# Threshold attention and SwiGLU: plain weight stores moved to later slots, with new transfer times and tables for the first batches

## The chip, the cores and the metric

The kernel runs on one core of a Trainium2 chip. The core has a matrix engine (TensorE, PE in the profile; its weight loads are PEld), a vector engine (VectorE, DVE), a scalar engine (ScalarE, ACT), a general engine (GpSimd, POOL) and SyncE (SP), which here only issues DMAs. Each engine takes its instructions in the order of the program and waits for the others by semaphores. The metric is the device time of one execution in microseconds; the median of several runs counts.

## What is computed

Eight batches of eight heads, with 576 tokens of 64 values a head. The attention keeps only the scores within tau of the largest of their row; its output is the input of a SwiGLU block with 512 inputs, 1536 hidden values and 512 outputs. All in float32.

```python
scores = scale * np.matmul(q, k.transpose(0, 1, 3, 2))
thresh = np.max(scores, axis=-1, keepdims=True) - tau
scores = np.where(scores >= thresh, scores, -1000000000.0)
scores = scores - np.max(scores, axis=-1, keepdims=True)
attn = np.exp(scores)
attn = attn / (np.sum(attn, axis=-1, keepdims=True) + 1e-09)
x = np.matmul(attn, v)               # then heads side by side: 4608 x 512
g = x @ w_gate
silu = g * (1.0 / (1.0 + np.exp(-g)))
out = (silu * (x @ w_val)) @ w_out
```

## The kernel before

**Head and slots.** The first batch is worked off by an older scheme (up to about 140 us), in which the weights are also fetched and brought to float32 form. After it the program is a chain of 84 slots. Seven batches have four pairs of heads each, and a pair takes three slots. In every slot PE computes scores (L1514) for a third of the queries of two heads. DVE takes the row maxima (L1535, L1537), the halves of a row are exchanged (by ACT, L1549, or by DVE, L1543), ACT takes exponentials (L1560), and DVE masks them and sums the rows (L1562). The reciprocal of the sum (L1576) scales the tiles, on ACT (L1588) or on POOL (L1585), and DVE transposes them (L1590). The scores lie in two PSUM tiles; the next slot's scores can start when the masks have read them. In the second slot of a pair PE first works off the attention products of the pair before (L1611).

**Loads.** In the first slot of a pair the q and k of the pair after it are loaded (L336, eight DMAs of 72 KB from SP); POOL scales q (L1650), DVE transposes k (L1652) and q (L1655). In the second slot v is loaded (L380).

**Work that fills a slot.** Between a slot's scores and the next, PE is given pieces of the SwiGLU block of the batch before. Batch 0 is done by plain products (`plain_group`, L1040, one step is eight matmuls of one matrix). Batches 1 and on use a Winograd form of Strassen's product with seven products instead of eight: six groups of columns (`Group`, L940, steps p1, p5, p2, p6, p3, p7, p4; after the first group p4 follows the next group's p1). The hidden values are multiplied with w_out in seven output products a half (`Outputs`, L1106; batches 0 and 1) or by a nested form (L1308, L1320; later batches).

**Sums of weights.** For the seven products each group needs three sums of weight blocks. POOL makes them in slots 4 to 9 (`weight_sums`, L795), and SP stores them to HBM (L847, 768 KB a group). A fourth sum replaces a weight block in place (`weight_part`, slots 10 to 15). In batch 1 a group takes four plain blocks from SBUF and its three sums from a ring of two places, to which they are loaded from HBM (`load_sums`, L867; the load for group g + 2 is asked for at p4 of group g). From batch 2 on all seven blocks of a group are streamed from HBM (`load_flow`, L873). For this the four plain blocks of each group have to be stored to HBM once as well: `store_plain` (L862), four DMAs of 256 KB a group. In this kernel it is called in slot 10 + g for group g.

**What sets the order.** A planner (`Plan`) keeps modelled clocks of the engines. Each operation is a job with an engine, a modelled duration, the jobs it depends on, a rank, and for DMAs two more values: `lag`, the time from issue to landing, and `moves`, the time that its bytes occupy the DMA engines; transfers with `moves` are queued one behind the other in the account. The planner emits jobs in the order in which they could start by the account, so a modelled time changes the order of the instructions on an engine, never what they do. PE's order is written by tables: how many steps a slot gets.

- `PLAIN` (slots 0 to 7): plain product steps of batch 0.
- `CH0` (slots 8 to 12): output products of batch 0.
- `GV` (slots of a batch from its second): group steps. One table for all batches.
- `CH`, `CD`: output products; `CH` for batches 0 and 1, of which the last rows fall into the first two slots of the batch after.
- `FIRST_POOLED`, `FIRST_MAX_BY_ACT` (slots 0 to 23): how many of the three tiles of the second head POOL scales, and in which slots ACT exchanges the maxima. `POOLED` and `MAX_BY_ACT` serve the later batches.

SP's queue is shared by all of this: q, k and v loads, the stores of sums and of plain blocks, the loads of the ring, the output. A DMA that waits on SP holds up all behind it.

Of the kernel before, what the change touches and what calls it, by code (L numbers as in the profile page):

```python
# [27 lines left out]
class Plan:  # L28
# [12 lines left out]
    def job(self, eng, took, fn, *deps, rank=1, lag=0.0, moves=0.0):  # L41
        j = Job(eng, took, fn, rank, lag, moves)
        for d in deps:
            if isinstance(d, Job) and d.end is None:
                d.then.append(j)
                j.waits += 1
            elif d is not None:
                j.ready = max(j.ready, self.after(d, eng) if isinstance(d, Job) else d + self.HOP)
        if not j.waits:
            self.open[eng].append(j)  # L50
        return j
# [61 lines left out]
def kernel(  # L113
# [11 lines left out]
    nc = tc.nc  # L125
# [15 lines left out]
    NU3 = 3  # L141
# [4 lines left out]
    NF2, DM2 = NF // 2, DM // 2  # L146
# [27 lines left out]
    HW = 2 * TC  # L174
# [15 lines left out]
    ring = big[:, 2 * NCC * DFF:].rearrange("p (s n) -> p s n", s=2)  # L190
# [11 lines left out]
    sums_hbm = hbm.tile([NF2, P, GW], F32, name="sums_hbm")  # L202
# [523 lines left out]
    plan = Plan()  # L726
    job, pe = plan.job, plan.pe
# [53 lines left out]
    def pair_cols(w, kh, g):  # L781
        return w[:, 2 * kh:2 * kh + 2, g * TC:(g + 1) * TC]
# [3 lines left out]
    SUM_AT = 2  # L786
# [7 lines left out]
    def pool_tt(out, a, b, op):  # L794
        return lambda: nc.gpsimd.tensor_tensor(out=out, in0=a, in1=b, op=op)  # L795
# [43 lines left out]
    stores, summed_g, parts = {}, {}, []  # L839

    def weight_sums(g, place, *deps):
        t1, t2, t4 = (place[:, n * HW:(n + 1) * HW].rearrange("p (k f) -> p k f", k=2) for n in range(3))
        w11, w12, w21, w22 = pair_cols(wval, 0, g), pair_cols(wgat, 0, g), pair_cols(wval, 1, g), pair_cols(wgat, 1, g)
        j = job("POOL", 1.3, pool_tt(t1, w12, w11, ALU.subtract), *deps, rank=3)
        j = job("POOL", 1.3, pool_tt(t2, w22, t1, ALU.subtract), j, rank=3)
        j = job("POOL", 1.3, pool_tt(t4, w21, t2, ALU.subtract), j, rank=3)
        stores[g] = job("SP", 0.1, lambda: nc.sync.dma_start(  # L847
            out=sums_hbm[g][:, SUM_AT * HW:(SUM_AT + 3) * HW], in_=place), j, lag=4.0)
        summed_g[g] = j

    def weight_part(g, *deps):
# [6 lines left out]
    def store_plain(g, *deps):  # L858

        js = []  # L860
        for n, w in ((0, pair_cols(wval, 0, g)), (1, pair_cols(wval, 1, g)), (5, pair_cols(wgat, 1, g)), (6, pair_cols(wgat, 0, g))):
            js.append(job("SP", 0.1, lambda n=n, w=w: nc.sync.dma_start(  # L862
                out=sums_hbm[g][:, n * HW:(n + 1) * HW].rearrange("p (k f) -> p k f", k=2), in_=w), *deps, lag=4.0))
        plain_stores[g] = js

    def load_sums(c, g, *deps):
        loads[c, g] = job("SP", 0.1, lambda: nc.sync.dma_start(  # L867
            out=ring[:, g % 2], in_=sums_hbm[g][:, SUM_AT * HW:(SUM_AT + 3) * HW]), stores[g], *deps, lag=4.0)

    def load_flow(c, g, part, *deps):  # L870
        lo, to = ((0, 4), (4, NQ))[part]
# [157 lines left out]
    def plain_group(t, g, n_bufs):  # L1029

        x = xts["full", t]

        def mul(mat, name):
            hold = take(name)

            def fn():
                ps = hold.rows()
                for i in range(2):
                    for c in range(NCC):
                        nc.tensor.matmul(ps[:, i], wgv[:, mat, c, (2 * g + i) * P:(2 * g + i + 1) * P], x[:, c, :],  # L1040
                                         start=(c == 0), stop=(c == NCC - 1))

            return hold, pe(2 * NCC * MM, fn, *hold.deps)

        hold, m = mul(0, "pg")
        (u, u_old), (n, n_old) = turn_of(u_bufs), turn_of(n_bufs)
        ps = hold.rows()
        tj = job("ACT", 0.6, lambda: nc.scalar.activation(n.ap, ps, AF.Tanh, scale=0.5), m, *n_old, rank=1)
        cj = job("ACT", 0.6, lambda: nc.scalar.activation(u.ap, ps, AF.Copy, scale=0.5), m, *u_old, rank=1)
        hold.read_by(tj, cj)  # L1050
        hold.done(False)
        yield
        hold, m = mul(1, "pv")
        ht, pv = hall[:, t, g], hold.rows()
        vj = job("DVE", 0.7, lambda: nc.vector.scalar_tensor_tensor(out=ht, in0=n.ap, scalar=1.0, in1=pv, op0=ALU.add, op1=ALU.mult),
                 tj, m, rank=1)
        n.jobs = [vj]
        hold.read_by(vj)
        hold.done(False)
        gated[0, t, g] = mj = job("POOL", 1.3, pool_tt(ht, ht, u.ap, ALU.mult), vj, cj, rank=1)  # L1060
        u.jobs = [mj]
        yield
# [634 lines left out]
    def end_gates():  # L1697
        state.pop("last_product")()

    def gv_steps(n):  # L1700
        for _ in range(n):
            next(state["gv"])
# [6 lines left out]
    NS = NU3 * NP  # L1709
    LAST_GV, LAST_PLAIN = 9, 8  # L1710
    GV = {1: 2, 2: 7, 3: 4, 4: 5, 5: 6, 6: 5, 7: 6, 8: 6, 9: 0}
    CH = {0: 2, 1: 5, 9: 1, 10: 3, 11: 2}
    POOLED = {1: 3, 3: 2, 6: 3, 7: 2, 11: 1}
    MAX_BY_ACT = (0, 3, 5, 6, 8, 9, 10)
    FIRST_POOLED = {0: 2, 1: 3, 3: 2, 4: 3, 6: 1, 7: 2, 8: 1, 10: 2, 11: 1, 12: 2, 13: 2, 16: 2, 17: 1, 19: 3, 20: 1, 22: 3, 23: 2}
    FIRST_MAX_BY_ACT = (1, 3, 5, 6, 9, 12, 14, 15, 17, 18, 20, 21, 23)
    CD = {0: 1, 1: 1, 9: 2, 10: 2, 11: 2}
    PLAIN = {0: 1, 1: 3, 2: 2, 3: 2, 4: 2, 5: 3, 6: 1, 7: 2}
    CH0 = {8: 3, 9: 2, 10: 4, 11: 3, 12: 2}

    def begin_outputs(c):
# [6 lines left out]
    def block_part(b, kk):  # L1728
        s = (b - 1) * NS + kk
        if s == 0:  # L1730
            state["gv"] = chain(*(plain_group(0, g, u_bufs) for g in range(IN_HEAD, NF2)), *(plain_group(1, g, n_bufs) for g in range(NF2)))
        if s <= NS:
            gv_steps(PLAIN.get(s, 0))
            if s == 2:
                first, state["run"] = outputs(0)
                first.half_sums(plan.t)
            elif s == LAST_PLAIN:
                next(state["gv"], None)
            out_steps(CH0.get(s, 0))
            return  # L1740
        c = b - 1
        if kk < 2 and state["run"]:
            out_steps((CH if c - 1 < DEEP else CD).get(kk, 0))
        if kk in GV:
            if kk == 1:
                state["gv"] = gates_and_values(c)
            gv_steps(GV[kk])
            if c == DEEP and kk <= len(NESTED):
                deepen(NESTED[kk - 1], plan.t, *(j for js in plain_stores.values() for j in js), *summed)
            if kk == LAST_GV:  # L1750
                next(state["gv"], None)
                begin_outputs(c)
                if c < DEEP:
                    out_steps(1)
                    end_gates()
        if kk >= LAST_GV:
            out_steps((CH if c < DEEP else CD).get(kk, 0))

# [3 lines left out]
    for s, (n, x) in enumerate((n, x) for n in range(len(halved)) for x in range(NU3)):  # L1762
        seg = halved[n]
        i, t = seg["i"], seg["tiles"][x]
        b, kk = s // NS + 1, s % NS
        if x == 1 and n > 0:
            prepare_v(seg, attend(halved[n - 1]))
        pss, mark = slot_scores(seg, t)
        if s == 0:
            next(last, None)  # L1770
            attend_tile()
            next(last, None)
            flip()
            plan.t += 2.4
            plan.free.update(DVE=2.0, ACT=2.5)
        elif s == 1:
            attend_tile()
            next(last, None)
            plan.t += 1.0
            store_last(0)  # L1780
        if s == 1:
            prepare_v(seg)
        at_, pooled, max_by_act = (kk, POOLED, MAX_BY_ACT) if b > DEEP else (s, FIRST_POOLED, FIRST_MAX_BY_ACT)
        slot_rest(seg, t, pss, mark, pooled.get(at_, 0), at_ in max_by_act, 1 if x == NU3 - 1 else 2)
        if x == 0 and n + 1 < len(halved):
            prepare_next(i + 1, plan.t)
        if s == 0:
            joins = rest_of_weights()
        block_part(b, kk)
        if 2 <= s < 6:  # L1790
            output_sums(s - 2, plan.t, *joins)
        if s in WS:
            g, place = WS[s]
            weight_sums(g, place, plan.t, *joins, stores.get({2: 0, 3: 1, 4: 3, 5: 4}.get(g)))
        if 10 <= s < 10 + NF2:
            g = s - 10
            weight_part(g, summed_g[g], plan.t)
            store_plain(g, parts[g])

    tail[0] = True  # L1800
    out_steps(1)
# [13 lines left out]
    for c in (B - 1, B):  # L1815
# [4 lines left out]
        if c < B:  # L1820
            w = SM // 2
            j = []
# [40 lines left out]
```

## Time and profile before

| what | value |
|---|---|
| median of 3 runs | 1403.74 us (1401.99 to 1404.30) |
| the profiled execution: time, span | 1406.35 us, 1404.5 us |
| mean granted clock of TensorE | 0.994 |
| matmuls: scores, group steps, attention, plain and output products | L1514, L940, L1611, L1040, L1106 |
| DMAs of SP: ring and stream loads (big<-sums_hbm) | 90, of 768 or 1024 KB |
| DMAs of SP: plain stores (sums_hbm<-big, 256 KB) | 24 |
| HBM read, written | 138.28 MB, 21.50 MB |

Slots 0, 13 and 26 begin at 140.89, 285.08 and 452.14 us of the span. The times of single instructions are from one profiled execution, whose span is the time from its first to its last instruction; 1.9 us of the device time lie outside it. Where a row names a releaser in brackets, the engine was idle before the instruction for that long, and the releaser is what ended the wait.

### The profile page before, as it was taken

Reading aid. Unit: us, or ns where it says so; the run is one execution under the profiler, and the core shown is the slowest. Engines: PE = TensorE matmul, PEld = TensorE weight load, DVE = VectorE, ACT = ScalarE, POOL = GpSimd, SP = SyncE. Lnnn points to the kernel's source line nnn. Section 1 sums busy time; section 2 is a strip of 40 time slices with the busy share of each in tenths; the row PEclk is TensorE's granted clock in tenths of the full one; section 3 lists DMA queues with packets and bytes.
Section 4 is the critical chain, followed back from the end, with each engine's and each line's share of the span. In section 5 each row is a group of like instructions: output and inputs, shape, how many; then the busy total and the mean of one; then the engine's idle time right before and its main releaser. Section 6 shows DMA issues by size and latency. Waiting matters only on the chain.

```text
span 1404.5 us, 38812 instructions
## 1 busy us (share of the span) xinstructions
PE 1365.8 (97%) x15486; PEld 1118.0 (80%) x15486; DVE 1023.4 (73%) x2680; ACT 867.4 (62%) x2257; POOL 693.3 (49%) x641
## 2 busy tenths in 40 slices
PE   9998999979999999999999999999999999999997
PEld 6666777758777778877888888887887788899897
DVE  7978888867787677787778777877777764365365
ACT  6878676666665677667667766776677773221320
POOL 2456598743375659733874378436943592000000
PEclk9999999999999999999999999999999999999999
DMA  7824305545324551545146523553065404424411
GB/s 170 217 93 154 82 19 142 185 131 139 81 77 114 140 140 36 165 127 146 35 131 157 144 58 108 146 142 93 27 196 141 110 26 151 144 78 143 152 51 31
DMA packets 208388, 162.30 MB, mean 116 GB/s; under 512 B 166224, under 2 KB 180560, under 8 KB 202832
## 3 DMA queue, kind: packets, MB, share of 16 engines
q1 hardware_dynamic: 204608, 159.39, 40.2%
q8 instruction: 123, 2.02, 0.6%
q10 hardware_dynamic: 3600, 0.43, 0.2%
q14 instruction: 57, 0.47, 0.1%
HBM read 138.28 MB, written 21.50 MB: 114 GB/s over the span
## 4 chain that ended last, share of the span: by engine, by line
PE 77%; DVE 1%; SPq 1%; issue 1%; DMA 0%; POOL 0%; ACT 0%; DVEq 0%; ACTq 0%
PE pb L940 17%; PE pa L940 12%; PE pe L940 12%; PE px L1308 11%; PE sc L1514 8%; PE xa L1611 8%; PE py L1320 5%; PE po L1106 3%; PE sc L940 1%; SPq L336 1%; DVE big L798 0%; PE sc L1308 0%; SPq L1370 0%; DVE hall L993 0%; DMA sums_hbm<-big 0%
## 5 line engine op out<-in xcount | busy, mean ns | idle before, releaser
L1562 DVE SCALAR_TENSOR_TENSOR pall<-sc,th,pall 128x288 f32<-128x288 f32 x504 | 243.6, 513 | 64.5 <-ACT pall L1560 50.4
L940 PE MATMUL pb<-xall,big 128*128 128x256 f32 x1080 | 256.5, 380 | 0.0
L1560 ACT ACTIVATE pall<-sc,nm 128x288 f32<-128x288 f32 x504 | 231.7, 497 | 34.3 <-DVE pall L1562 33.9
L1590 DVE STREAM_TRANSPOSE pall<-pall 128x576 f32<-128x576 f32 x252 | 189.1, 763 | 62.6 <-ACT pall L1588 44.2
L940 PEld LDWEIGHTS pb<-xall,big 128*128 128x128 f32 x1080 | 203.7, 190 | 29.9 <-issue 2.7
L1588 ACT ACTIVATE pall<-pall,ri 128x288 f32<-128x288 f32 x416 | 189.7, 526 | 24.6 <-DVE ri L1576 24.1
L795 POOL TENSOR_TENSOR hall<-hall,tmp 128x512 f32<-128x512 f32 x80 | 102.3, 1279 | 167.0 <-DVE hall L993 157.7
L940 PE MATMUL pa<-xall,big 128*128 128x256 f32 x768 | 183.4, 382 | 0.0
L940 PE MATMUL pe<-xall,big 128*128 128x256 f32 x752 | 179.2, 381 | 0.2 <-POOL xall L795 0.2
L1514 PE MATMUL sc<-kT,qT 64*32 64x144 f32 (+1 forms) x5376 | 153.6, 350 | 15.2 <-DVE pall L1562 10.3
L940 PEld LDWEIGHTS pa<-xall,big 128*128 128x128 f32 x768 | 143.9, 190 | 22.8 <-issue 3.4
L940 PEld LDWEIGHTS pe<-xall,big 128*128 128x128 f32 x752 | 141.8, 190 | 22.1 <-issue 2.7
L1514 PEld LDWEIGHTS sc<-kT,qT 64*32 64x32 f32 x5376 | 100.9, 107 | 69.4 <-issue 31.3
L1535 DVE TENSOR_REDUCE mx<-sc 128x2 f32<-128x576 f32 x168 | 124.4, 740 | 35.4 <-PE sc L1514 35.0
L1611 PE MATMUL xa<-pall,vall 64*32 64x288 f32 x4032 | 133.7, 404 | 1.8 <-issue 1.0
L1585 POOL TENSOR_SCALAR pall<-pall,ri 128x288 f32<-128x288 f32 x88 | 88.1, 1013 | 68.7 <-DVE ri L1576 56.9
L1611 PEld LDWEIGHTS xa<-pall,vall 64*32 64x32 f32 x4032 | 76.0, 107 | 52.7 <-issue 9.2
L1570 ACT COPY sums<-sums 32x6 f32<-32x6 f32 x336 | 66.6, 198 | 45.5 <-DVE pall L1562 40.9
L992 ACT ACTIVATE vall<-tmp 128x512 f32<-128x512 f32 x96 | 60.4, 629 | 55.2 <-DVE tmp L1005 29.9
L1320 PE MATMUL py<-wo,hall 128*128 128x256 f32 x336 | 74.8, 379 | 0.0
L1549 ACT COPY mx<-mx 32x6 f32<-32x6 f32 x192 | 37.3, 194 | 60.5 <-DVE mx L1537 58.6
L1537 DVE TENSOR_REDUCE mx<-sc 128x1 f32<-128x288 f32 x168 | 74.4, 443 | 0.0
(225 smaller groups left out, 2326.9 us busy)
## 6 DMA issues: line engine op xcount, KB each, us to landing
big<-sums_hbm SPq DMA_DIRECT2D x42, 1024.0 KB, 5.3
big<-sums_hbm SPq DMA_DIRECT2D x48, 768.0 KB, 4.7
vall<-in_v_dram SPq DMA_DIRECT2D x112, 144.0 KB, 3.1
out_dram<-big SPq DMA_DIRECT2D x32, 256.0 KB, 3.5
qT<-in_q_dram SPq DMA_DIRECT2D x112, 72.0 KB, 4.8
kT<-in_k_dram SPq DMA_DIRECT2D x112, 72.0 KB, 3.0
wo<-in_moe_w_gate_dram SPq DMA_DIRECT2D x16, 384.0 KB, 3.8
wo<-in_moe_w_val_dram SPq DMA_DIRECT2D x16, 384.0 KB, 4.6
```

The source lines that it names most:

```text
L795: return lambda: nc.gpsimd.tensor_tensor(out=out, in0=a, in1=b, op=op)
L940: nc.tensor.matmul(ps[:, i], w[:, k_, i * P:(i + 1) * P], x[:, k_, :], start=first and i == k_ == 0, stop=True, skip_group_check=True)
L1308: nc.tensor.matmul(ps, a[:, f, :], ws[n][:, f, :], start=bank_ not in begun, stop=True, skip_group_check=True)
L1320: nc.tensor.matmul(ps, a[:, f, i * P:(i + 1) * P], operands[o][:, f, :], start=first and i == f == 0, stop=True, skip_group_check=True)
L1514: nc.tensor.matmul(pss[h][(slice(g * G, (g + 1) * G), *part)], qT[hs, col:col + G], kT[hs, c * SH + keys[0]:c * SH + keys[1]], start=True, ...
L1535: rs.append(job("DVE", 0.72, lambda n=n, tile_=tile_: nc.vector.tensor_reduce(out=mx[:, n:n + 2, 0], in_=tile_[:, :, 0:SH], axis=AX.X, op= ...
L1560: ej = job("ACT", 0.42, lambda x=x, n=n: nc.scalar.activation(ps[x], scs[x], AF.Exp, bias=nm[:, n:n + 1]), ej, *((masks[h, 0], masks[h, 1] ...
L1562: masks[x] = job("DVE", 0.45, lambda x=x, n=n: nc.vector.scalar_tensor_tensor(out=ps[x], in0=scs[x], scalar=th[:, n:n + 1], in1=ps[x], op0 ...
L1585: scaled.append(job("POOL", 1.02, lambda x=x, n=n: nc.gpsimd.tensor_scalar(out=x, in0=x, scalar1=ri[:, n:n + 1], scalar2=None, op0=ALU.mul ...
L1588: scaled.append(job("ACT", 0.46, lambda x=x, n=n: nc.scalar.activation(x, x, AF.Copy, scale=ri[:, n:n + 1]), rj, rank=rank))
L1590: seg["turned"].append(job("DVE", 0.72, lambda both=both: nc.vector.transpose(out=both, in_=both), *scaled, rank=rank))
L1611: nc.tensor.matmul(holds[a].ap()[x * G:(x + 1) * G, 0:SH].rearrange("d (i q) -> d i q", q=G), vr[rs, h, j, ds], p[rs, h, :, j, :], start=( ...
```

## The change

Three things are changed. Plain blocks are stored later: group g is no longer stored in slot 10 + g, but groups 0 to 5 in slots 13, 14, 16, 17, 19 and 20, which are the slots of batch 1 that load no q and k. The account of the planner gets other values for the stores and loads of sums (shorter `lag`, and `moves`, which they lacked), and 0.6 us of issue for a plain store. The tables are written anew: `GV_FIRST` serves batch 1 in place of `GV`; `CH`, `PLAIN`, `FIRST_POOLED` and `FIRST_MAX_BY_ACT` have other entries. The sums of the PE tables are the same as before: 41 group steps, 16 plain steps, 14 output products a batch.

```diff
@@ weight_sums
         stores[g] = job("SP", 0.1, lambda: nc.sync.dma_start(
-            out=sums_hbm[g][:, SUM_AT * HW:(SUM_AT + 3) * HW], in_=place), j, lag=4.0)
+            out=sums_hbm[g][:, SUM_AT * HW:(SUM_AT + 3) * HW], in_=place), j, lag=2.0, moves=3.4)
@@ store_plain
-            js.append(job("SP", 0.1, lambda n=n, w=w: nc.sync.dma_start(
-                out=sums_hbm[g][:, n * HW:(n + 1) * HW].rearrange("p (k f) -> p k f", k=2), in_=w), *deps, lag=4.0))
+            js.append(job("SP", 0.6, lambda n=n, w=w: nc.sync.dma_start(
+                out=sums_hbm[g][:, n * HW:(n + 1) * HW].rearrange("p (k f) -> p k f", k=2), in_=w), *deps, lag=2.0, moves=1.3))
@@ load_sums
         loads[c, g] = job("SP", 0.1, lambda: nc.sync.dma_start(
-            out=ring[:, g % 2], in_=sums_hbm[g][:, SUM_AT * HW:(SUM_AT + 3) * HW]), stores[g], *deps, lag=4.0)
+            out=ring[:, g % 2], in_=sums_hbm[g][:, SUM_AT * HW:(SUM_AT + 3) * HW]), stores[g], *deps, lag=1.6, moves=3.4)
@@ tables
     GV = {1: 2, 2: 7, 3: 4, 4: 5, 5: 6, 6: 5, 7: 6, 8: 6, 9: 0}
-    CH = {0: 2, 1: 5, 9: 1, 10: 3, 11: 2}
+    GV_FIRST = {1: 4, 2: 5, 3: 4, 4: 6, 5: 7, 6: 3, 7: 6, 8: 6, 9: 0}
+    CH = {0: 2, 1: 3, 10: 4, 11: 4}
     POOLED = {1: 3, 3: 2, 6: 3, 7: 2, 11: 1}
     MAX_BY_ACT = (0, 3, 5, 6, 8, 9, 10)
-    FIRST_POOLED = {0: 2, 1: 3, 3: 2, 4: 3, 6: 1, 7: 2, 8: 1, 10: 2, 11: 1, 12: 2, 13: 2, 16: 2, 17: 1, 19: 3, 20: 1, 22: 3, 23: 2}
-    FIRST_MAX_BY_ACT = (1, 3, 5, 6, 9, 12, 14, 15, 17, 18, 20, 21, 23)
+    FIRST_POOLED = {1: 3, 2: 2, 3: 2, 4: 3, 5: 1, 7: 2, 8: 2, 9: 1, 10: 2, 11: 1, 12: 1, 13: 3, 15: 3, 16: 3, 18: 3, 19: 1, 20: 1, 21: 3, 22: 1, 23: 3}
+    FIRST_MAX_BY_ACT = (1, 2, 3, 6, 9, 12, 14, 15, 16, 17, 18, 20, 21, 22)
     CD = {0: 1, 1: 1, 9: 2, 10: 2, 11: 2}
-    PLAIN = {0: 1, 1: 3, 2: 2, 3: 2, 4: 2, 5: 3, 6: 1, 7: 2}
+    PLAIN = {0: 2, 1: 2, 2: 3, 3: 1, 4: 2, 5: 3, 6: 1, 7: 2}
@@ block_part
-            gv_steps(GV[kk])
+            gv_steps((GV_FIRST if c == 1 else GV)[kk])
@@ the loop over slots (s: slot, x: place of the slot in its pair, NS = 12, NU3 = 3)
             weight_part(g, summed_g[g], plan.t)
-            store_plain(g, parts[g])
+        if s > NS and x and (g := (s - NS) * (NU3 - 1) // NU3) < NF2:
+            store_plain(g, parts[g], plan.t)
```

## The prediction, made before the changed kernel ran

> **What bounds the kernel now.** I read the page's busy line first, then who PE waited for, then PE's instructions in order of time, and last a table by stage with one row a slot.
>
> ```profile
> PE 1365.8 (97%) x15486; PEld 1118.0 (80%) x15486; DVE 1023.4 (73%) x2680; ACT 867.4 (62%) x2257; POOL 693.3 (49%) x641
> ...
> PE sc L1514 <- DVE pall L1562: 10.3, 3, 7.5
> PE sc L1514 <- issue: 3.3, 2, 1.7
> ```
>
> PE is the bound: it is idle for 1404.5 - 1365.8 = 38.7 us. The two lines of waits (engine and line waiting, releaser, us in total, times, longest) are those of PE from 141 to 455 us, which is slots 0 to 25. Beyond slot 26 the instruction lists of the two programs are the same on PE, DVE and ACT, so all that the change can win lies in this stretch. There PE waits before a slot's scores (L1514): for the masks of the slot before (L1562), which free the PSUM tiles.
>
> ```profile
> 140.89:151.03 10.14, 7.60 (x109) 5.68 (x108) 8.91 (x27) 8.00 (x16) 3.04 (x2) 1.00 0.39 58
> 151.03:166.11 15.08, 15.08 (x132) 12.03 (x132) 12.31 (x31) 9.03 (x26) 9.14 (x6) 0.89 0.36 102
> 166.11:176.53 10.42, 8.82 (x98) 7.10 (x97) 8.70 (x27) 6.55 (x17) 6.09 (x6) 1.00 0.36 58
> ...
> 285.08:298.41 13.33, 5.62 (x89) 3.98 (x73) 8.64 (x25) 5.44 (x15) 7.55 (x8) 0.87 0.91 269
> 298.41:314.38 15.97, 15.97 (x121) 13.03 (x121) 11.56 (x32) 11.97 (x34) 5.06 (x5) 0.90 0.05 7
> ...
> 413.33:422.08 8.75, 7.09 (x89) 5.57 (x89) 7.40 (x23) 5.23 (x15) 8.14 (x11) 1.00 0.09 32
> ```
>
> One row a slot, from scores to scores (slots 0, 1, 2, 13, 14, 23): length, busy us of PE, PEld, DVE, ACT, POOL, PE's clock, DMA share, GB/s. A slot without disturbance needs some 8.7 to 9.1 us for its chain of maxima, exponentials and masks (slot 23: 8.75, slot 4: 9.12); where PE has less work than that it waits. Slot 13 is the bad one: PE has 5.62 us of work, the slot lasts 13.33, and the clock is 0.87, and 0.90 in the slot after. Its cause is seen on SP and DVE:
>
> ```profile
> 269.30 4.83 SPq L867 DMA_DIRECT2D big<-sums_hbm  x2
> 274.18 3.66 SPq L862 DMA_DIRECT2D sums_hbm<-big  x4
> 277.89 4.80 SPq L336 DMA_DIRECT2D qT<-in_q_dram  x4
> 282.73 3.00 SPq L336 DMA_DIRECT2D kT<-in_k_dram  x4
> ...
> 289.22 0.78 DVE L1652 STREAM_TRANSPOSE kT<-kT 128x576 f32<-128x576 f32 x1 [4.83 <-DMA kT<-in_k_dram]
> 289.92 0.73 DVE L1655 STREAM_TRANSPOSE qT<-qT 128x576 f32<-128x576 f32 x1
> ...
> 298.41 3.58 PE L1514 MATMUL sc<-kT,qT 64*32 64x288 f32 x64 [7.48 <-DVE pall L1562]
> 301.92 1.99 PE L940 MATMUL pa<-xall,big 128*128 128x256 f32 x8
> ```
>
> The q and k of the next pair of heads are issued behind the plain stores of group 1 (L862), so k lands at 289.2; DVE, which has its transposes ahead of slot 13's maxima, waits 4.83 us, and PE 7.48. The scores after that take 3.58 us where other slots take 1.72.
>
> **What the skill says.** "DMA: Bandwidth & Descriptors", Anatomy of one DMA: a semaphore wait of a DMA happens on the issuing sequencer before dispatch. The SP rows agree: the 4.83 us of L867 are a wait for PE and POOL, and all behind it is late. "Perfetto Trace Analysis", Tensor Engine Instruction: ACT, DVE and GPSIMD are strict FIFO. The trace agrees: DVE's maxima stand 4.83 us behind a transpose they don't need. "TensorE: Matmul & The Clock Gate", What's actually happening: the array falls to half clock after an idle window of about 3.4 us and is released after as much work. The trace agrees on the factor (3.58 against 1.72) but shows it after a gap of only 2.54 us too (3.57, slot 1); gaps of 1.60 and 1.66 gave 2.13.
>
> **Part by part.** What slots 0 to 25 lose now: gaps of 2.54 (before slot 1), 1.60 (3), 0.31 (5), 0.23 (in 13), 7.48 (14), 0.51 (15) and 1.66 (24), together 14.3; slow scores 3.57 - 1.72 and 3.58 - 1.72, and twice 2.13 - 1.72, 4.5 in all. Sum 18.9.
>
> (1) Plain stores, 24 DMAs of 256 KB, leave slots 10 to 15 for slots 13 to 20. In the new list of SP the order at slot 12 is: store of the sums of group 4, ring load for group 0 (L867), then q and k. The ring load still waits for product five of the second token half (PE at 273.7). So q and k go out from about 274.1 instead of 277.9, with one 768 KB load before them instead of 1 MB of stores and two such loads. Each DMA waits for the eighth before it (eight semaphores in turn in the list); the last k waits for that ring load, 4.7 us median to landing, 278.5. With 3.0 to 4.8 us to land, k is there at 282 and q, scaled on POOL in 1.72, at 283. DVE reaches its transposes at 284.4: no wait. In slot 13 the maxima start at 286.8 rather than 291.2. Price of the moved stores where they go: they stand between ring loads, and the list has, for slots 14 to 16: load for group 2 (waits for PE, about 304 by the old clock), 1 MB of stores, then q and k, whose last DMAs wait for those stores. The two sizes, 1.8 MB, need 5.3 us at the 340 GB/s that the crowded stretch from 262 us showed; k lands near 315 and its transpose stands ahead of slot 16's maxima at about 319. Cover 4 us, and slot 16 has 12 us of PE work over its chain of 9, another 3. I take 0; range 0 to 9.3 (the old stall over again).
>
> (2) The new modelled times move no instruction's duration. They put the k transpose of slots 15, 18 and 22 later in DVE's queue. I take 0 of their own; what they give is in (1).
>
> (3) Tables. PE's work to the next scores, from 3.45 us a plain product, 2.6 an output product, 1.73 a group step, 4.4 an attention step and 1.65 the scores: slot 0 goes from 8.5 to 11.9, slot 1 from 13.0 to 9.6, slot 2 from 8.6 to 12.0, slot 3 from 12.9 to 9.5, slot 13 from 5.1 to 8.6, slot 14 from 13.8 to 10.3, slot 21 from 13.0 to 10.4, slot 23 from 6.8 to 12.1, slot 25 from 18.1 to 12.9. Work is the same in sum. Slot 0's chain ended 10.14 after its scores, so 2.54 + 1.85 go. Slot 2's took 10.42: 1.60 + 0.41 go. Slot 23's 8.75: 1.66 + 0.41 go. What is late next:
> - Slot 1. ACT's new list has six scalings of slot 0 (6 x 0.46) behind a copy of xlast that waits for the attention tile of slot 1, and ahead of the exchange of maxima. From scores at 152.0: copy 155.1, scalings to 157.8, exchange to 158.6, six masks and two transposes to 163.3, against PE ready at 161.8. I take 1.4 + 0.4; between 0 and 3.
> - Slot 13. L981, which waits for the fourth group step (end 293.8), stands ahead of the last mask: that ends at 295.2 and scores start at 295.3. I take 1.5 + 0.4; between 0.3 (chain alone) and 3.5 + 1.9 (clock at half).
> - Slots 3, 4, 14: 0.2, 0.3, 0.5. The 0.51 before slot 15's attention stays. For slots 15 to 25, with POOL scaling three tiles in five of them, 1.2 for waits I can't place; 0 to 4.
> Eight more scalings go to POOL (41 for 33): 8 x 1.01 on POOL, which is idle for half the span, and 8 x 0.53 off ACT; neither is the bound.
>
> New losses 1.8 + 1.9 + 1.0 + 0.5 + 1.2 = 6.4; gain 18.9 - 6.4 = 12.5 us. The profiled execution took 1406.35 with a span of 1404.5, so 1393.9 for such a run; off the median 1403.74 it is 1391.2. I say 1391.
>
> **Rivals.** *A, forecast*: as summed, 1386 to 1396. Chance 0.57.
> *B, half of it*: k comes in time, but the short slots 1, 3, 13 and 14 each wait 2 to 3 us, because the chain, not the transfer, was the limit there: for it, slot 13 has 8.6 us of work to a chain with two transposes and L981 in it; against, slots 4 and 7 with 8.6 of work wait 0.3. Losses 12 to 13 instead of 6.4: 1397.5. Chance 0.20.
> *C, no gain*: the ring load for group 0 holds up SP as the stores did, q and k still land near 288, and the stall of 7.5 stays, while the new waits eat the 6.5 us of slots 0, 2 and 23. For it: old SP sat in that load for 4.83. Against: it is released at 273.7, before the old issue. 1403. Chance 0.10.
> *D, slower*: stores and ring loads alternate in slots 14 to 19, where SP waits for PE at each ring load; if q and k of slots 15 and 18 then land over 7 us later than I have (after 322 by the old clock), DVE stalls at both as it did before slot 13: 2 x 9.3 = 18.7 lost against 12.5 won, 1410. For it: k at 315 took up to 5.4 us to land with half those stores around. Against: 7 us of cover. Decides from about 13 us of stall. Chance 0.13.
> That the tables don't do what they say is excluded: PE's list shows the steps moved.
>
> **The numbers.** Under 0.2% (2.8 us, about what a measurement of this kernel can tell) counts as the same. A and B are faster, a third of C too: 0.80; the rest of C, 0.07, the same; D 0.13 slower. Low end: all of the 18.9 but 1 us gone, 1386. High end 1403 takes in B and most of C; D is left out. A's own range is 1386 to 1396.
>
> **What would show it.** Right: no DVE wait on k near slot 13; that slot some 10 us long; gaps before slots 1, 3 and 24 gone; the clock 1.00 throughout slots 0 to 25; small new gaps before slots 2 and 14; PE busy down by some 4 us with the clock, idle by 8. Wrong: a DVE wait for k or q in slots 15 to 19 (D); SP's q and k after slot 12 issued later than 277 by the old clock (C); gaps of over 2 us before slots 2, 4 and 14 (B).

## The result and the profile after

The changed kernel takes 1387.78 us (median of four runs, 1386.28 to 1387.92) against 1403.08 (four runs, 1401.99 to 1404.30): a ratio of 0.9888, with a 95% interval of 0.9871 to 0.9905. That is 15.3 us less where 12.5 were predicted, 1387.8 for the 1391 forecast. Its profiled execution took 1387.66 with a span of 1385.9, and PE is busy for 1360.6 us of it. So PE's idle time fell from 38.7 to 25.3 us, and its busy time by 5.2.

Who PE waited for in slots 0 to 25 and beyond, from 141 to 455 us, in the profile of the changed kernel (engine and line waiting, releaser: us in total, times, longest):

```profile
PE sc L1514 <- DVE pall L1562: 2.2, 3, 1.6
PE xa L1611 <- PE pv L1040: 0.2, 1, 0.2
```

Before, the first of these lines had 10.3 us, and a second one 3.3. The table by stage, one row a slot (slots 0, 1, 2, 13, 14, 23; length, then busy us of PE, PEld, DVE, ACT, POOL, PE's clock, DMA share, GB/s):

```profile
140.95:151.94 10.99, 10.99 (x125) 8.73 (x124) 9.78 (x30) 8.82 (x18) 3.04 (x2) 1.00 0.37 54
151.94:163.22 11.28, 9.70 (x118) 7.84 (x118) 10.85 (x25) 8.26 (x25) 7.26 (x4) 1.00 0.48 137
163.22:175.83 12.61, 12.61 (x112) 10.34 (x112) 11.71 (x33) 9.90 (x28) 6.36 (x5) 1.00 0.30 48
280.83:289.81 8.98, 8.81 (x104) 7.10 (x89) 7.52 (x24) 6.46 (x17) 4.49 (x6) 1.00 0.79 221
289.81:301.52 11.71, 11.16 (x105) 8.86 (x105) 9.84 (x26) 8.51 (x23) 6.30 (x6) 1.00 0.27 84
399.95:412.16 12.21, 12.21 (x114) 10.11 (x113) 10.27 (x32) 6.17 (x17) 8.57 (x13) 1.00 0.23 62
```

Slots 0, 2 and 23 are now filled by PE's own work. Slot 13 is 8.98 us long where it was 13.33, with 8.81 us of work in it, and the clock is 1.00 in every row. Slots 13 and 14 together shrank from 29.30 to 20.69: this pair alone is 8.6 of the 15.5 us by which slot 26 starts earlier. SP's queue and DVE's transposes around slot 13 show why:

```profile
269.58 0.33 SPq L867 DMA_DIRECT2D big<-sums_hbm  x1
269.95 2.65 SPq L336 DMA_DIRECT2D qT<-in_q_dram  x4
272.65 3.67 SPq L336 DMA_DIRECT2D kT<-in_k_dram  x4
276.42 0.57 SPq L847 DMA_DIRECT2D sums_hbm<-big  x1
```

```profile
280.14 0.78 DVE L1652 STREAM_TRANSPOSE kT<-kT 128x576 f32<-128x576 f32 x1
280.84 0.73 DVE L1655 STREAM_TRANSPOSE qT<-qT 128x576 f32<-128x576 f32 x1
```

The q and k leave SP 7.9 us earlier than before (269.95, not 277.89). Of this, 4.2 us are the earlier start of slot 13 (280.83, not 285.08); counted from that start they leave 3.7 us earlier. The transposes carry no bracket: DVE waits for neither. No DVE instruction waits for a DMA anywhere in slots 0 to 25.

### The profile page after: what moved, and what is told of

The parts are those of the page before. It is cut to its first block, busy times and chain, and to the rows that moved or that the text cites. A ratio compares the mean times of both kernels' runs of the same rounds, so it can differ in the third digit from the quotient of the medians.

```text
span 1385.9 us, 38809 instructions
## 1 busy us (share of the span) xinstructions
PE 1360.6 (98%) x15486; PEld 1115.8 (81%) x15486; DVE 1024.4 (74%) x2676; ACT 867.0 (63%) x2253; POOL 701.0 (51%) x649
## 4 chain that ended last, share of the span: by engine, by line
PE 90%; DVE 4%; ACT 2%; DMA 1%; SPq 1%; issue 1%; ACTq 0%; DVEq 0%
PE pb L940 17%; PE pa L940 12%; PE pe L940 12%; PE px L1308 12%; PE sc L1514 10%; PE xa L1611 9%; PE po L1106 5%; PE py L1320 5%; PE pg L1040 2%; PE pv L1040 2%; PE sc L940 1%; PE pv L517 1%; SPq L336 1%; DMA vall<-in_v_dram 1%; PE xa L500 1%
## 5 line engine op out<-in xcount | busy, mean ns | idle before, releaser
L1588 ACT ACTIVATE pall<-pall,ri 128x288 f32<-128x288 f32 x408 | 186.6, 527 | 25.0 <-DVE ri L1576 24.3
L795 POOL TENSOR_TENSOR hall<-hall,tmp 128x512 f32<-128x512 f32 x80 | 103.7, 1296 | 160.1 <-DVE hall L993 144.7
L1514 PE MATMUL sc<-kT,qT 64*32 64x144 f32 (+1 forms) x5376 | 149.2, 345 | 2.9 <-DVE pall L1562 2.2
L1514 PEld LDWEIGHTS sc<-kT,qT 64*32 64x32 f32 x5376 | 97.8, 106 | 56.4 <-issue 20.2
L1585 POOL TENSOR_SCALAR pall<-pall,ri 128x288 f32<-128x288 f32 x96 | 96.0, 1014 | 63.0 <-DVE ri L1576 62.9
```

The costliest lines, as they stand in the source:

```text
L1514: nc.tensor.matmul(pss[h][(slice(g * G, (g + 1) * G), *part)], qT[hs, col:col + G], kT[hs, c * SH + keys[0]:c * SH + keys[1]], start=True, ...
L1585: scaled.append(job("POOL", 1.02, lambda x=x, n=n: nc.gpsimd.tensor_scalar(out=x, in0=x, scalar1=ri[:, n:n + 1], scalar2=None, op0=ALU.mul ...
L1588: scaled.append(job("ACT", 0.46, lambda x=x, n=n: nc.scalar.activation(x, x, AF.Copy, scale=ri[:, n:n + 1]), rj, rank=rank))
```

## The experiments

Every kernel is the one before or the changed one with one part different. Times are compared with runs of the kernel before on the same chip (medians 1402.42, 1402.97 and 1403.89 in the three groups).

**The stores alone.** The kernel before, with

```
-            store_plain(g, parts[g])
+        if s > NS and x and (g := (s - NS) * (NU3 - 1) // NU3) < NF2:
+            store_plain(g, parts[g], plan.t)
```

> The kernel before, with the plain stores moved to slots 13 to 20 and nothing else. Theory: the move by itself brings q and k in time, so DVE no longer waits for k ahead of slot 13's maxima; but with the old tables PE has 5.6 us of work in that slot against a chain of some 9, so 3 to 4 us of the 7.48 us gap stay, with some of the slow scores. The losses before slots 1, 3 and 24 stay. 3 to 6 us faster than before: about 1399 where before is 1403. Rival 1: the stall was the transfer alone, gap and slow scores both go: 9.3 us faster, about 1394. Rival 2: the two ring loads of 768 KB that still stand ahead of q and k keep k late: under 1 us faster.

Measured: 1400.97 (21 runs), ratio 0.9988 (0.9981 to 0.9994), 1.4 us faster. Its slots 13 and 14:

```profile
283.48:292.46 8.98, 5.36 (x88) 4.06 (x73) 8.06 (x25) 5.44 (x15) 5.41 (x7) 1.00 0.73 227
292.46:308.61 16.15, 16.15 (x120) 12.51 (x120) 11.40 (x32) 11.88 (x34) 4.97 (x5) 0.89 0.05 7
```

k comes in time, and slot 13 falls to its chain of 8.98. But PE has only 5.36 us to do in it, so a gap of 3.62 stays, the clock falls just as it did after 7.48 (0.89 where it was 0.90), and slot 14 is no shorter: 16.15 for 15.97. In the profile the pair of slots gains 4.2 of the 8.6 us. The timed runs give less, 1.4, under the 3 to 6 that I expected; the last pair of experiments below has to do with that.

**The tables alone.** The kernel before with all five new tables, stores and modelled times as they were:

> The kernel before with all five new tables; stores and modelled times as they were. Theory: slots 0, 2 and 23 give their 8.5 us (2.54 + 1.85, 1.60 + 0.41, 1.66 + 0.41), slot 1 takes 2.0 back, and slot 13's end is still set by k, whose wait on DVE stays at 3 us or more; but the 3.5 us of work that the table moves from slot 14 into slot 13 now lie inside that wait, so slot 14 is shorter by as much. 8.5 - 2.0 + 3.5 = 10 us faster than before, between 7 and 12. Rival: the gap before slot 14 stays near 7 us and the tables give 6.5 or less.

Measured: 1393.98, ratio 0.9936 (0.9923 to 0.9948), 8.4 us faster. Its slots 13 and 14:

```profile
280.44:294.59 14.15, 9.70 (x105) 7.24 (x90) 8.77 (x25) 6.45 (x17) 6.72 (x7) 1.00 0.93 263
294.59:307.27 12.68, 12.63 (x105) 9.41 (x105) 9.04 (x25) 8.49 (x23) 6.30 (x6) 0.87 0.07 14
```

Here k is late (DVE waits 5.63 us for it), PE's gap is 4.15, and the work moved from slot 14 into slot 13 lies inside the stall: the two slots take 26.83, 2.5 less than before. So the move and the tables gain 4.2 and 2.5 in these slots when alone and 8.6 together, counted from one profile of the kernel before. Each leaves a gap of 3.6 to 4.2, by the other's cause, and with the gap the low clock behind it.

**All but PE's tables.** The changed kernel with the old `PLAIN` and `CH` and without `GV_FIRST`:

```
-    GV_FIRST = {1: 4, 2: 5, 3: 4, 4: 6, 5: 7, 6: 3, 7: 6, 8: 6, 9: 0}
-    CH = {0: 2, 1: 3, 10: 4, 11: 4}
+    CH = {0: 2, 1: 5, 9: 1, 10: 3, 11: 2}
...
-    PLAIN = {0: 2, 1: 2, 2: 3, 3: 1, 4: 2, 5: 3, 6: 1, 7: 2}
+    PLAIN = {0: 1, 1: 3, 2: 2, 3: 2, 4: 2, 5: 3, 6: 1, 7: 2}
```

> The changed kernel with the three old tables of PE's work (plain products, output products, group steps); moved stores, new modelled times and the two new tables of scalings and maxima kept. Theory: it loses slots 0, 2 and 23 again (8.5), and 3 to 4 us at slot 13 because PE has too little to do there, and gets back the 2.0 of slot 1 and 1.3 of slot 14: 8 to 10 us slower than the changed kernel, 5 to 7 faster than before. Rival: the tables of PE are worth only slots 0, 2 and 23 less what they cost, 5 us slower than the changed kernel.

Measured: 1401.81 (13 runs), ratio 0.9993 (0.9985 to 1.0001). Some 14 us are lost against the changed kernel, more than the 8 to 10 expected, and what is left can't be told from no gain. In its profile slots 0 to 25 alone take 12.9 us more than in the changed kernel. The gaps of 2.53, 1.31 and 1.30 before slots 1, 3 and 24 are back, and 3.62 before slot 14 with scores of 3.79; slots 13 and 14 together lose 4.9. DVE does not wait for k. In slot 24 there is a gap that no other kernel here has; no other has PE's old tables beside POOL's new ones:

```profile
425.28 4.70 PE L1611 MATMUL xa<-pall,vall 64*32 64x288 f32 x144 [1.84 <-ACT pall L1560]
```

Another 2.2 us lie beyond slot 26, where I had looked for nothing; see the pauses below.

**All but POOL's tables.** The changed kernel with the old `FIRST_POOLED` and `FIRST_MAX_BY_ACT`:

> The changed kernel with the old tables of scalings on POOL and of maxima through ACT. PE's list is the same; on SP both ring loads now stand ahead of the q and k of slot 12, as they do in the kernel with the old modelled times. Theory: the tables themselves cost little, under 1 us over slots 0 to 12 and 15 to 25; but k lands late in slot 13 as it did there, so 1 to 4 us slower than the changed kernel, with DVE waiting for k. Rival: the scalings were worth something of their own, and gaps of over 1 us in sum come up before slots other than 2 and 14.

Measured: 1387.32, ratio 0.9884 (0.9863 to 0.9905): not to be told from the changed kernel. The expectation fell. The first ring load leaves at 264.23, five us ahead of the second, and k is transposed at 279.91 without a wait. Both loads stood in front of q here too, as in the kernel with the stores alone (267.10 and 272.24, k in time); beside the next experiment, this points to their leaving at once as what delays k. These two tables are worth nothing that can be measured here.

**All but the modelled times.** The changed kernel with the old times of stores and ring loads (the plain stores too go back to 0.1 and `lag=4.0`):

```
-            out=sums_hbm[g][:, SUM_AT * HW:(SUM_AT + 3) * HW], in_=place), j, lag=2.0, moves=3.4)
+            out=sums_hbm[g][:, SUM_AT * HW:(SUM_AT + 3) * HW], in_=place), j, lag=4.0)
...
-            out=ring[:, g % 2], in_=sums_hbm[g][:, SUM_AT * HW:(SUM_AT + 3) * HW]), stores[g], *deps, lag=1.6, moves=3.4)
+            out=ring[:, g % 2], in_=sums_hbm[g][:, SUM_AT * HW:(SUM_AT + 3) * HW]), stores[g], *deps, lag=4.0)
```

> The changed kernel with the old modelled times of stores and ring loads. On SP this issues both ring loads and both late sums ahead of the q and k of slot 12, and in DVE's queue the k transposes of later pairs stand before the reduction of the slot's sums instead of behind. Theory (the new times are worth nothing of their own, since transfers are over 4 us ahead of need): within 1 us of the changed kernel. Rival: q and k land behind two ring loads and DVE waits at its transposes in slot 13 or 16, 2 us or more slower than the changed kernel.

> The changed kernel with the old modelled times once more, for a second profile. Its first profiled run took 1392.66 with k late by 3.2 us on DVE; its five runs lay between 1386.38 and 1392.66. Theory: the landing of k varies from run to run by several us, so this run, if it is shorter, shows a smaller wait for k and a smaller gap before slot 14, and only that differs. Rival: the wait is 3.2 again within 0.5 us whatever the total, and the spread comes from elsewhere.

Measured: 1389.81 (five runs, 1386.38 to 1392.66), ratio 0.9905 (0.9887 to 0.9922); its interval and that of the changed kernel overlap. The two profiled executions of this one program took 1392.66 and 1387.10. Slots 13 and 14 of the first, and DVE's transpose of k in it:

```profile
280.88:292.59 11.71, 8.81 (x104) 7.16 (x89) 8.76 (x25) 6.46 (x17) 6.07 (x7) 0.98 0.71 211
292.59:306.76 14.17, 14.12 (x105) 10.37 (x105) 9.22 (x25) 8.56 (x23) 6.30 (x6) 0.77 0.06 10
```

```profile
283.40 0.78 DVE L1652 STREAM_TRANSPOSE kT<-kT 128x576 f32<-128x576 f32 x1 [3.20 <-DMA kT<-in_k_dram]
```

The same of the second:

```profile
280.40:289.61 9.21, 8.80 (x104) 7.12 (x89) 8.76 (x25) 6.45 (x17) 4.47 (x6) 1.00 0.74 230
289.61:301.22 11.61, 11.16 (x104) 8.87 (x105) 9.05 (x25) 8.51 (x23) 6.30 (x6) 1.00 0.07 9
```

```profile
280.42 0.78 DVE L1652 STREAM_TRANSPOSE kT<-kT 128x576 f32<-128x576 f32 x1 [0.71 <-DMA kT<-in_k_dram]
```

In both, SP sends two ring loads at once at 269, then q and k; the four k issues take 6.32 us in the first and 4.55 in the second, against 3.67 in the changed kernel, which sends one load there, and 3.00 and 3.22 in the two kernels that send the two loads five us apart. In the second k is transposed 3.0 us earlier, in a slot that starts only 0.5 earlier, and the pair of slots takes 20.82 instead of 25.88: 5.1 of the 5.6 us between the two executions. So k's landing does differ from run to run. With the old modelled times it lies on the edge of being needed. With the new ones and the new tables of PE, in the changed kernel and the five others here that have both, no profile shows a wait for k in slot 13. The median fits the rival, 2 us or more, but the overlap of the intervals leaves it open. Nor is it the new times by themselves that space the loads: with PE's old tables they too leave at once (271.73), the k issues take 7.28 us, and DVE is spared the wait because its list has the transpose later (289.50).

**Double stores.** In the changed kernel each plain store is issued a second time, the same bytes to the same place:

```
+            js.append(job("SP", 0.6, lambda n=n, w=w: nc.sync.dma_start(
+                out=sums_hbm[g][:, n * HW:(n + 1) * HW].rearrange("p (k f) -> p k f", k=2), in_=w), *deps, lag=2.0, moves=1.3))
```

> The changed kernel with every plain store issued twice (48 DMAs of 256 KB for 24, the same bytes to the same place), so 2 MB of stores between ring loads where there was 1 MB; the result is the same. It tests the price of the moved stores in slots 14 to 20. Theory: k for slots 15 and 18 was ready 4 us or more ahead of need, so even doubled stores give no wait over 1 us on PE: within 1.5 us of the changed kernel. Rival (the prediction's slower case): q and k stand behind 2 to 3 MB on SP, DVE waits for k in slot 16 or 19, and PE loses 5 to 9 us at each.

Measured: 1388.21 (1387.17 to 1392.26), ratio 0.9896 (0.9877 to 0.9916). The test was harder than meant: SP sends each repeat only 2.5 to 6 us after its first, so the next pair's q leaves at 314.41, not 302.67, and its k is still transposed without a wait (323.45). In slots 0 to 25 DVE waits once for a k, 1.1 us. Slot 20 is longer by 0.40, and slot 13 by 0.83, as it is by 0.7 to 1.0 in the three kernels on slot 1 below, which have no double stores; what grows in slot 13 are the scores, 2.26 to 2.54 us for 1.70, with a pause of PE of up to 0.2 us inside them, for which the trace names no wait. The slower rival of the prediction falls with the time of the changed kernel itself; here q left 11.7 us later at no price that shows in the profile. Two of the five runs took 1391.51 and 1392.26, some 4 us over the median, and no profile shows why.

**Slot 1: what is late there.** Three kernels. In the first, three of slot 0's six scalings go from ACT to POOL (`FIRST_POOLED = {0: 3, 1: 3, ...`):

> The changed kernel with three of slot 0's six scalings given to POOL, which takes 3 x 0.45 us off ACT ahead of the exchange of maxima in slot 1; nothing else moves. The prediction's account of slot 1 (ACT's six scalings make the exchange late): the gap of 1.58 us before slot 2 shrinks by 1.2 to 1.6 and the slow scores go, 1.2 to 2 us faster. Theory now: DVE's maxima come late, because the weight join L832 stands ahead of them and takes 1.99 us; ACT already waits 0.66 us for them, so the gap stays at 1.4 us or more and the time within 0.4 us.

In the second, the weight join L832 and the add L834 have `rank=3` for `rank=2`, which puts the join behind slot 1's masks:

> The changed kernel with the weight join and the add after it at a lower priority in the account, so that L832 comes after slot 1's masks and not ahead of its maxima; a transpose of k (0.76) takes its place. Theory: maxima end at about 156.9 instead of 158.0; then ACT's scalings (end 157.5) are the next to be late, so the gap before slot 2 falls from 1.58 to about 0.9, and its scores by up to 0.4: 0.7 to 1.2 us faster. Rival (ACT is the limit alone): the gap stays within 0.2.

The third has both:

> Both edits together: the join behind slot 1's masks and three scalings of slot 0 on POOL. Theory: neither DVE's maxima nor ACT's scalings are then late; the gap before slot 2 is 0.6 us or less, the scores of slot 2 take 1.7, and the time is 1.2 to 2 us below the changed kernel, more than the two edits alone give together. Rival: POOL's 3 x 1.0 us push its scaling of q or the gating behind, and a new wait takes the gain: within 0.4 us.

Measured: 1388.32 (ratio 0.9893, 0.9879 to 0.9908), 1388.96 (0.9897, 0.9880 to 0.9913) and 1388.88 (0.9898, 0.9883 to 0.9912). None beats the changed kernel. The gaps before slot 2 are 1.57, 0.93 and 0.86, against 1.58. The timeline of the changed kernel in slot 1 (start, duration, engine, line, out<-in, and in brackets the idle time before and its releaser):

```profile
153.41 1.83 POOL L834 TENSOR_TENSOR wo<-wo,extra 128x768 uint32<-128x768 uint32 x1 [7.07 <-ACT sums L1570]
...
154.06 1.99 DVE L832 SCALAR_TENSOR_TENSOR wo<-extra,wo 128x768 uint32<-128x768 uint32 x1
...
154.82 2.67 ACT L1588 ACTIVATE pall<-pall,ri 128x288 f32<-128x288 f32 x6
155.18 2.00 POOL L795 TENSOR_TENSOR hall<-hall,tmp 128x512 f32<-128x512 f32 x1
155.97 0.75 DVE L1535 TENSOR_REDUCE mx<-sc 128x2 f32<-128x576 f32 x1
...
158.14 0.81 ACT L1549 COPY mx<-mx 32x6 f32<-32x6 f32 x4 [0.66 <-DVE mx L1537]
```

ACT in the kernel with three scalings on POOL:

```profile
154.71 1.39 ACT L1588 ACTIVATE pall<-pall,ri 128x288 f32<-128x288 f32 x3
158.02 0.81 ACT L1549 COPY mx<-mx 32x6 f32<-32x6 f32 x4 [1.93 <-DVE mx L1537]
```

ACT is done 1.3 us sooner and waits 1.3 us longer: the exchange starts at 158.02 for 158.14, in a slot that starts 0.11 earlier. So the scalings are not what is late. The maxima stand behind a join that takes 1.99 us where it takes 0.95 just before. With the join moved away the gap falls to 0.93, as expected, and then ACT's scalings are next: the exchange follows them without a wait. With both edits it falls no further than 0.86. In that profile ACT waits 0.57 us for DVE's L1553, the last step of the maxima, which stands behind two transposes (1.42 us from 156.81); no run moved these. Moving the join also costs: the maxima of slot 3 come later, PE waits 1.57 us for ACT's exchange there, and slot 3 takes 11.30 for 9.90. The 0.65 is given back twice over.

**Pauses with nothing to wait for, and the spread of the kernel before.** Two single runs, one of the kernel before unchanged, one with `run_idle(10)` for `run_idle(6)` at its start:

> The kernel before once more, for a second profile. The first profiled run took 1406.35 where the median of the timed runs is 1402 to 1403. Theory: the landing of k in slot 12 to 13 differs from run to run, and with it DVE's wait ahead of slot 13 (4.83 us in the first profile); this run, if nearer the median, shows a wait 2 to 4 us shorter and the rest of the slots as they were. Rival: the wait is 4.83 again within 0.5 us, and the 3 us are somewhere else (clock, start, end).

> The kernel before with four more idle matrix products at the very start (eight more rows of the trace), inside PE's first wait of 1.7 us; nothing else differs. The three kernels with PE's old tables pause in the same places with nothing to wait for: 0.5 us after the 8th of the 144 rows of the second tile's attention in slots 15 and 27, and 0.7 us after the 26th of 64 rows of the scores of slot 67; the three with the new tables have none of the three. Theory: the pause belongs to a place in PE's stream of instructions (its supply), so with eight rows more ahead of it it falls eight rows earlier in the work: at the start of the attention and after about the 18th row of the scores. Rival: it belongs to a wait that the trace doesn't name, and stays at the 8th and the 26th row.

The second profile of the kernel before took 1405.57, with 4.5 us of wait for k and a gap of 6.97, near the first, as the rival said; it was no nearer the median, so the theory was not put to the test. The third, with four more idle products, took 1401.46, and its wait for k is 2.31. PE's pauses in the first profile of the kernel before:

```profile
476.02 4.33 PE L1611 MATMUL xa<-pall,vall 64*32 64x288 f32 x132 [0.50 <-issue]
520.06 0.69 PE L1514 MATMUL sc<-kT,qT 64*32 64x144 f32 x24 [0.76 <-issue]
961.87 1.17 PE L1514 MATMUL sc<-kT,qT 64*32 64x288 f32 x38 [0.71 <-issue]
```

In the one with eight more rows at the start:

```profile
473.30 4.33 PE L1611 MATMUL xa<-pall,vall 64*32 64x288 f32 x132 [0.51 <-issue]
516.77 0.72 PE L1514 MATMUL sc<-kT,qT 64*32 64x144 f32 x32 [0.43 <-issue]
```

A row such as x132 is what follows the pause. There are two kinds. The pause in the attention stays at the same matmul, 132 from the end of the row: it belongs to a wait that the trace doesn't name (the rival). The two kernels in slot 27, before and changed:

```profile
474.82 0.69 PE L1611 MATMUL xa<-pall,vall 64*32 64x288 f32 x8
475.40 0.59 ACT L1015 ACTIVATE tmp<-pb 128x512 f32<-128x512 f32 x1
```

```profile
459.30 4.60 PE L1611 MATMUL xa<-pall,vall 64*32 64x288 f32 x144
459.88 0.59 ACT L1015 ACTIVATE tmp<-pb 128x512 f32<-128x512 f32 x1
```

Before, PE goes on at 476.02, and L1015, which halves a product of a group step and copies it out of PSUM, ended at 475.99. So it is in slots 15 and 27 of all five profiles with PE's old tables: PE goes on 0.03 to 0.04 us after L1015 ends. In the nine profiles with the new tables L1015 ends 0.9 us after that matmul, and PE waits for nothing. `take` in the kernel gives each product the PSUM tile that the modelled clocks say is free first. So the likely account is that with the old tables the attention's second product was given the tile that L1015 still reads. The trace shows no tile numbers, and this was not run by itself.

The pause in slot 31's scores falls eight rows earlier, 32 from the end and not 24, so it belongs to a place in PE's stream. The one in slot 67, which was expected to move in the same way, is gone. With it slot 67 takes 12.19 instead of 13.53.

## Why the prediction was right, and where it was off

**Sign and cause: right.** k in time, slot 13 near 10 us or less, the gaps before slots 1, 3 and 24 gone, the clock at 1.00: each is in the profile. The case with half the gain asked for gaps of over 2 us before slots 2, 4 and 14; they are 1.58, none and 0.67 (in two pieces). The case without gain asked for q and k to leave SP after 277 by the old clock, that is, by the times of the profile before. They left at 269.95; slot 13 starts 4.25 us earlier now, so this is 274.2 by the old clock. The slower case fell by the time itself.

**Parts (1) and (2), stores and modelled times.** Set back by the same 4.25 us, the prediction's path through slot 13 holds to a tenth of a us: q leaves at 269.95 (said 274.1, so 269.85), k is transposed at 280.14 (280.15) and the maxima start at 282.60 (282.55). One reading was inexact: the 4.83 us of L867 hold a wait of 3.8 for PE and none for POOL. "I take 0" for where the stores go is confirmed with room. "I take 0 of their own" for the modelled times can't be called wrong: the time without them is 2.0 us higher but the intervals overlap. What the profiles show is that together with the tables of PE they space the two ring loads, and that without them one of two executions had the stall back in part. Joining stores and tables into one sum hid that neither of them alone gets at slot 13 what both get together.

**Part (3), tables.** Slots 0, 2 and 23 gave what was priced. Slot 1 cost 1.58 + 0.41 where 1.4 + 0.4 was taken, but for the wrong reason: the step "six masks and two transposes" after ACT's "scalings to 157.8, exchange to 158.6" took ACT as the limit and DVE as ready. The size came out by chance, since a join of 1.99 us on DVE happened to end its maxima 0.6 us behind ACT's scalings. Without the join the scalings leave 0.93, not 1.4. Two terms were too large. Slot 13's 1.5 + 0.4 was 1.28 in all. The rows of DVE and PE at its end:

```profile
289.68 0.70 DVE L981 TENSOR_TENSOR pb<-pb,tmp 128x512 f32<-128x512 f32 x1
289.81 0.64 PE L1514 MATMUL sc<-kT,qT 64*32 64x288 f32 x2 [0.18 <-DVE pall L1562]
290.28 0.51 DVE L1562 SCALAR_TENSOR_TENSOR pall<-sc,th,pall 128x288 f32<-128x288 f32 x1
290.95 1.69 PE L1514 MATMUL sc<-kT,qT 64*32 64x288 f32 x62 [0.49 <-DVE pall L1562]
```

The path is the one that was predicted: L981 stands ahead of the last mask, PE is done at 289.64 (293.9 by the old clock, 293.8 was said), and all but two rows of the scores begin at 290.95 (295.2, said 295.3). But two rows ran inside the wait, and the 0.4 for slow scores had no ground, as the 62 rows took 1.69. The "1.2 for waits I can't place" had nothing in it, nor had the 0.51 before slot 15's attention. One loss came that was not foreseen: slot 15's scores at 2.35, 0.63 over 1.72; its cause is open. And scores of 2.13 are not the mark of a gap of 1.6 or of a low clock, as the prediction reads them: in both kernels slots 5 and 8 have 2.13 too, after gaps of 0.31 at most and at a clock of 1.00.

**The sum.** From profile to profile the gain is 18.7 (1406.35 to 1387.66), so 6.2 were missed, half of them on each side of slot 26. New losses in slots 0 to 25 are 1.99 + 1.28 + 0.63 = 3.9, not 6.4. That is 2.5 of the gain that was missed; another 0.4 is slot 16, whose scores take 1.70 for 2.11, which the prediction did not price. In all, slots 0 to 25 gave 15.6.

Another 3.1 came beyond. There the prediction took the lists to be the same and concluded that "all that the change can win lies in this stretch", slots 0 to 25. This step failed. In slot 27 ACT's list is not the same. Before, four scalings (L1588, from 478.60) stand ahead of the copies of the attention products (L1622, 480.32). In the changed kernel one does (463.08; L1622 at 463.94), and three follow (464.62). And a list by names leaves out which PSUM tile a product is given, on which PE's pause in that slot seems to hang. Slot 27 takes 13.14 for 13.88 and slot 28 10.46 for 10.87, 1.15 us together; all five profiles with PE's old tables have the longer figures and all nine with the new ones the shorter. The other 2.0 are pauses inside scores whose length differs from profile to profile: slot 67 takes 12.29 for 13.53, slots 31 and 64 are shorter by 0.4 each. These can't be put down to the tables: slot 67 takes 12.19 with the old tables and four more idle products, and 12.83 with the new tables and three scalings on POOL.

**Off the median.** The last step of the sum had an error of the other sign. The profiled execution of the kernel before took 1406.35, some 3 us over its median, and its gaps were counted in full and then taken off the median. From median to median the gain is 15.3, not 18.7. So 6.2 too little and 3.4 too much cancel in part, and that 1391 came so near 1387.8 is in part luck. What differs between executions is shown in part: k's landing (waits of 4.83, 4.5 and, in the kernel with four more idle products, 2.31), the clock in slot 1, and the pause in slot 67. That these make up the whole 3 us is not shown. Timed runs agree as to the clock: of the 33 runs of the kernel before in the first group, the 14 with a mean granted clock of at most 0.993 took 1404.0 us on average, the 12 with at least 0.995 took 1401.6. In the execution of 1401.46 us slots 13 and 14 take 27.59 us and not 29.30, so measured from that one the changed kernel gains 6.9 us in this pair rather than 8.6, and the stores alone 2.5 rather than 4.2.

## What to carry to other kernels

A stall with two causes, a late transfer and too little work behind it, gives back less to the two cures taken singly than to both: here 4.2 and 2.5 us of 8.6, since a gap of 3.62 was followed by scores of 3.78 us, and one of 7.48 by 3.58. When a slot is refilled, list for each engine what stands ahead of the first instruction of the critical chain, with the time that it takes beside its new neighbours, before naming the engine that is late. Where a planner orders the work and hands out buffers, compare the lists of the two programs to their ends, buffers included, before a stretch is called untouched. And before an event's cost is taken off a median, ask whether the profiled run is a median run: a transfer that lands near the moment it is needed shows up in some executions only.

## What the runs showed of the hardware

**DVE and POOL block each other.** The join L832 reads two operands from SBUF. It took 0.95 us with POOL idle, and 1.99 when POOL's add L834 was running: the add ended at 155.24 and the join at 156.05. POOL's next operation, L795, begun at 155.18, then took 2.00 for its usual 1.28. "SBUF — State Buffer", Who interferes with whom, of the Trainium skill says that a DVE instruction with two SBUF inputs contends with a GpSimd instruction that reads SBUF, and that the ports they share are an exclusive lock. That whoever issues first holds them for the whole instruction it says of another mode of DVE. The numbers agree with both: the join lost 1.04 us, and POOL's add had 1.18 left when the join began; L795 lost 0.72, and the join had 0.87 left. With the join moved it took 1.07, and the L795 that began 0.23 us after it 1.97.

**The clock after a gap is not a fixed price.** The gap of 2.54 us before slot 1 cost slow scores and a clock of 0.89 in both profiles of the kernel before, but not in the kernel that differs by four idle products at the start. The rows of slot 1, first the second profile of the kernel before, then that kernel:

```profile
151.20:166.30 15.10, 15.10 (x132) 12.00 (x132) 12.33 (x31) 8.73 (x25) 9.15 (x6) 0.89 0.37 102
```

```profile
151.75:165.25 13.50, 13.50 (x133) 11.00 (x133) 12.44 (x31) 9.15 (x26) 8.47 (x6) 1.00 0.41 115
```

The same work, after gaps of 2.53 and 2.54, takes 15.10 or 13.50 (the scores in it 3.54 or 2.14): 1.6 us hang on something other than the length of the gap. The page "TensorE: Matmul & The Clock Gate", What's actually happening, of the skill calls the window of about 3.4 us in which activity is judged free-running, not tied to the kernel; two outcomes of one gap agree with that. That a gap of 2.5 is enough at all does not agree with the page's full idle window, and there the measurement decides. No run here shows the window itself.

**Pauses by place.** PE pauses for 0.2 to 0.8 us inside the scores of slot 31 in every profile, with nothing to wait for: after 38 to 41 of the 64 rows in thirteen profiles, and after 32 in the one with eight rows more at the start. What supplies the stream and why it stops there is open.
